# Block-sparse attention and a gated layer in one plan: another load order, wider transposes and masks, and a plan with other durations

## The chip, the cores and the metric

The kernel runs on one core of one Trainium2 chip. The core has five engines that work side by side, each with its own stream of instructions in a fixed order: PE (TensorE, matrix products; its weight loads are listed apart as PEld), DVE (VectorE), ACT (ScalarE), POOL (GpSimd) and SP (SyncE, which only issues DMAs here). They wait for each other through semaphores. PE writes to PSUM, which has eight banks of 128 partitions by 512 fp32 values; the other data lies in SBUF. DMAs are issued by SP and ACT, and by POOL where a transfer also converts fp32 to fp16.

The metric is the device time of one execution in microseconds, as the median over runs. Traces show one profiled execution, in microseconds from its first instruction.

## The reference

Four sequences (batch 4) with 8 heads, 768 positions and 64 values a head go through attention with a block mask, and the result, as 3072 tokens of 512 values, through a gated layer with 2048 hidden values.

```python
scores = scale * np.matmul(q, k.transpose(0, 1, 3, 2))
blk_i, blk_j = pos[:, None] // 32, pos[None, :] // 32
mask = np.abs(blk_i - blk_j) <= 1
mask = mask | (blk_i == 0) | (blk_j == 0) | (blk_i == 23) | (blk_j == 23)
for qb in range(24):
    for kb in sampled_blocks[qb]:          # three drawn blocks
        mask[qb*32:(qb+1)*32, kb*32:(kb+1)*32] = True
scores = np.where(mask, scores, -1e9)
attn = softmax(scores)
x = (attn @ v) as [3072, 512]
h = x @ w_in                               # [3072, 2048]
g = h * (1 / (1 + exp(-beta * h)))
out = g @ w_out                            # [3072, 512]
```

## The kernel before

**Tiling.** The 24 blocks of 32 positions of a sequence fall into two kinds. Blocks 0 and 23 see all keys ("global rows"). The other 22 see eight blocks each: three drawn ones, the first, their three neighbours and the last. They are done in 11 pairs a sequence, 44 pairs in all, named by n; g is the block within the pair, u the head within one of four head pairs hp.

**A pair's way.** `kg` on POOL (line 710) copies the six drawn key blocks into KG by offsets read from the input, `kn` (lines 714 to 732, the copy itself on the helper's line 330) the neighbours. `sc` on PE first writes the mask into two PSUM banks (line 849: a product of ones with a row that holds a large negative number where a drawn block repeats another one) and adds the scores (line 862). `mx` on DVE takes row maxima (line 884), `ex` on ACT the exponentials and their sums (line 892), `nrm` on POOL or DVE divides (line 915) from the 12th pair on; the first 11 pairs, called late, divide after the product by a factor that `hl` prepares (lines 902 to 904) and PE spreads (line 953). `tp` transposes the weights on PE (line 929; from pair 31 on by a DMA, line 933), `ptv` copies them out of PSUM, `av` multiplies by the gathered V blocks (line 971, from pair 16 on line 963), `xv` stores the result into xT.

**V.** Sequence V is rearranged into Vn, written to a table VT in DRAM (line 659), and gathered from it into VG by DMAs on SP (line 810). For the first four pairs the drawn V blocks come out of a product with a selection matrix on PE instead (`pick`, line 825). The V tiles of pairs 4 to 7 lie in g1, the second of the two buffers that later hold g.

**Preparation of a sequence.** Raw K and Q are loaded with 128 partitions of six positions each, cast to fp16 (line 538, first sequence only; the others are cast by POOL's DMAs of line 588), transposed per head pair on PE, one head at a time into half of the partitions (`trK`, `trQ`, line 632), and copied into KT and QT (`evK`, `evQ`, Q times the scale).

**Dense layers.** Tokens go in eight groups G of 256 or 512. `h` (line 1155) multiplies by w_in, `tanh` on ACT (line 1161) and `stt` on DVE (line 1166) form g, `y` (line 1182) multiplies by w_out, `oe` scales into osb, and SP stores. Weights are loaded by POOL's DMAs (lines 557, 563), which wait for a tiny POOL copy (`touch`, line 543) that waits for a V gather of pair 2.

**What sets the order.** Everything is a task in a list planner (class Plan). A task names its engine or engines, a duration, what it depends on, the banks that it opens and closes, and a priority. `Plan.run` simulates the engines, the banks and two DMA rings, and starts on each free engine the ready task of least priority plus OFFSET, a table of names. The tasks are then emitted in that order; the chip keeps it on each engine. A wrong duration does not change a result, only what stands ahead of what.

## Time and profile before

| what | value |
|---|---|
| median of 3 runs | 302.34 us (300.25 to 303.63) |
| profiled execution | span 302.9 us; no other time is given for it |
| PE busy | 279.5 us, 92% |
| DVE busy | 237.5 us, 78% |
| ACT busy | 218.6 us, 72% |
| POOL busy | 170.0 us, 56% |
| mean granted clock of PE | 0.981 |
| moved by DMA | 47.55 MB |

A row of the table of stretches gives the stretch, its length, then for PE, PEld, DVE, ACT and POOL the busy time with the count of instructions in brackets, and at the end the granted clock of PE, the share of the DMA engines and GB/s. A row of the timeline gives the start, the time from the first start to the last end, engine and line, operation, what is written and read with shapes, the count, and in brackets the idle time of the engine before it and what ended it. A row of waits names who waited for whom, the sum, the times and the longest. A row of groups has busy time and the mean of one in ns behind the first bar. PE's matmuls overlap, so a busy PE is not PE at full speed.

### The profile page before, as it was taken

To read this page: it belongs to the slowest core of one execution; us is meant where nothing else is said; L and a number is where in the kernel's file an instruction comes from. 1 tells how busy PE (TensorE), PEld (TensorE's weight loads), DVE (VectorE), ACT (ScalarE), POOL (GpSimd) and SP (SyncE) were. 2 spreads that over 40 slices of the span, in tenths; PEclk is the share of its full clock that TensorE was granted. 3 is DMA by queue.
4 is the path that set the end of the run, shared out by engine and by line. 5 is a ranking of instruction groups with operands and counts; after the bars stand their busy time and mean duration, and the time that the engine had idled before them with its cause. 6 is when DMAs were issued, how large, how long until landed. Compare 5 with 4: busy or idle time off the path is not lost.

```text
span 302.9 us, 11451 instructions
## 1 busy us (share of the span) xinstructions
PE 279.5 (92%) x4109; PEld 173.8 (57%) x4109; DVE 237.5 (78%) x556; ACT 218.6 (72%) x641; POOL 170.0 (56%) x513
## 2 busy tenths in 40 slices
PE   2599879999998799999999999999999999999993
PEld 1465668758846576665556555545554544555671
DVE  5848987999899998999999739999888834762150
ACT  3357657888789598799889749896787768763360
POOL 5057995034579957899777538677976654000000
PEclk9999957999999999999999999999999999999999
DMA  7999999979978852299933643248465446541102
GB/s 248 365 294 171 205 232 231 228 142 265 213 126 167 181 192 72 84 173 162 237 99 106 202 154 106 67 110 167 120 158 119 126 106 181 137 121 53 53 36 69
DMA packets 57170, 47.55 MB, mean 157 GB/s; under 512 B 19733, under 2 KB 53142, under 8 KB 57114
## 3 DMA queue, kind: packets, MB, share of 16 engines
q1 hardware_dynamic: 44736, 35.48, 41.3%
q0 software_dynamic: 12320, 11.27, 24.7%
q8 instruction: 32, 0.52, 0.7%
q14 instruction: 24, 0.20, 0.2%
q10 hardware_dynamic: 58, 0.07, 0.1%
HBM read 45.23 MB, written 9.44 MB: 180 GB/s over the span
## 4 chain that ended last, share of the span: by engine, by line
PE 49%; DVE 23%; issue 7%; ACT 6%; POOL 6%; DMA 5%; POOLq 2%; SPq 0%; DVEq 0%; ACTq 0%
PE bank L1155 17%; PE bank L1182 14%; DVE ST L884 5%; PE bank L825 4%; DVE g L1166 4%; PE bank L929 3%; POOL KG L710 3%; DMA g<-in_k_dram 3%; DVE SG L1040 3%; POOL PP L915 2%; PE bank L963 2%; PE bank L971 2%; ACT PP L892 2%; PE bank L632 2%; ACT t L1161 2%
## 5 line engine op out<-in xcount | busy, mean ns | idle before, releaser
L1155 PE MATMUL bank<-xT,w_in_sb 128*128 128x256 f16 (+1 forms) x512 | 93.8, 330 | 1.5 <-DVE g L1166 1.5
L892 ACT ACTIVATE PP<-bank,ST 128x256 f16<-128x256 f32 x176 | 81.9, 482 | 15.1 <-DVE ST L884 10.1
L1182 PE MATMUL bank<-w_out_sb,g 128*128 128x512 f16 x384 | 92.0, 379 | 0.0
L1161 ACT ACTIVATE t<-bank,beta_sb 128x512 f16<-128x512 f32 (+1 forms) x128 | 71.0, 595 | 15.7 <-PE bank L1155 10.4
L915 POOL TENSOR_SCALAR PP<-PP,ST 128x256 f16<-128x256 f16 x132 | 63.4, 499 | 30.8 <-DVE ST L909 29.2
L1166 DVE SCALAR_TENSOR_TENSOR g<-t,bank 128x512 f16<-128x512 f16 (+1 forms) x128 | 67.0, 547 | 16.3 <-ACT t L1161 15.8
L1155 PEld LDWEIGHTS <-w_in_sb 128*128 128x128 f16 x512 | 54.4, 115 | 28.1 <-issue 4.1
L710 POOL COPY KG<-KT 128x64 f32 x264 | 52.4, 249 | 25.6 <-PE bank L862 10.5
L884 DVE TENSOR_REDUCE ST<-bank 128x2 f32<-128x512 f32 x88 | 57.6, 680 | 4.2 <-PE bank L862 3.8
L1182 PEld LDWEIGHTS <-g 128*128 128x128 f16 x384 | 35.0, 98 | 37.4 <-issue 3.5
L892 ACT ACTIVATION_READ_ACCUMULATOR PP<-bank,ST 128x1 f32 x176 | 37.4, 212 | 0.0
L1061 POOL TENSOR_SCALAR PG<-PG,SG 128x768 f16<-128x768 f16 x13 | 13.1, 1010 | 24.4 <-ACT PG L1049 15.2
L334 ACT ACTIVATE osb<-bank 128x512 f32<-128x512 f32 (+1 forms) x24 | 14.2, 590 | 16.1 <-PE bank L1182 16.0
L330 DVE COPY PT<-bank 128x1024 f16<-128x1024 f16 x30 | 20.4, 683 | 3.8 <-PE bank L929 3.6
L330 DVE CAST xT<-bank 64x256 f16<-64x256 f32 (+1 forms) x35 | 14.6, 418 | 9.9 <-PE bank L963 6.8
L929 PE MATMUL bank<-identity,PP 128*128 128x128 f16 x248 | 20.4, 225 | 1.2 <-ACT KT L328 0.6
L963 PEld LDWEIGHTS <-VG 128*128 128x128 f16 x448 | 16.1, 98 | 9.2 <-issue 4.3
L1049 ACT ACTIVATE PG<-bank,SG 128x384 f16<-128x384 f32 x32 | 18.3, 589 | 4.2 <-DVE SG L1042 3.6
L929 PEld LDWEIGHTS <-PP 128*128 128x128 f16 x248 | 16.2, 101 | 6.0 <-issue 1.1
L963 PE MATMUL bank<-PT,VG 128*128 128x64 f16 x448 | 17.5, 193 | 2.2 <-DMA PT<-PP 1.5
L330 POOL COPY KG<-KT 128x384 f32<-128x384 f32 (+3 forms) x43 | 16.6, 411 | 1.3 <-PE bank L862 1.3
L328 ACT CAST xT<-bank 64x256 f16<-64x256 f32 (+1 forms) x30 | 11.3, 375 | 8.2 <-PE bank L1089 3.9
(119 smaller groups left out, 317.9 us busy)
## 6 DMA issues: line engine op xcount, KB each, us to landing
VG<-VT SPq DMA_DIRECT2D x220, 32.0 KB, 2.6
VG<-VT SPq DMA_DIRECT2D x32, 192.0 KB, 2.7
out_dram<-osb SPq DMA_DIRECT2D x20, 256.0 KB, 2.1
RV<-in_v_dram POOLq DMA_DIRECT2D x6, 384.0 KB, 6.6
RK<-in_k_dram POOLq DMA_DIRECT2D x6, 384.0 KB, 6.2
VT<-Vn SPq DMA_DIRECT2D x3, 768.0 KB, 3.4
RQ<-in_q_dram POOLq DMA_DIRECT2D x6, 384.0 KB, 6.3
w_in_sb<-in_moe_w_in_dram POOLq DMA_DIRECT2D x8, 256.0 KB, 8.8
```

Of the source, the lines that this page charges most:

```text
L330: (nc.vector if eng == "DVE" else nc.gpsimd).tensor_copy(out=out, in_=in_)
L710: nc.gpsimd.tensor_copy(out=kg32[:, g, :, (SR + r) * W:(SR + r + 1) * W], in_=kt32[:, :, bass.ds(vals[3 * g + r], W)])
L884: mx[n, u] = add(f"mx{n}.{u}", "DVE", 0.6, lambda n=n, u=u, sb_=sb_: nc.vector.tensor_reduce(out=sb_[:, 0, 2 * u:2 * u + 2], in_=bank(("S" ...
L892: nc.scalar.activation(out=pb[:, u, g, :], in_=bank(("S", n, u))[:, g * 256:(g + 1) * 256], func=AF.Exp, bias=sb_[:, 0, 2 * u + g:2 * u + ...
L915: (nc.vector if eng == "DVE" else nc.gpsimd).tensor_scalar(out=pb[:, u, g, :], in0=pb[:, u, g, :], scalar1=sb_[:, 2, 2 * u + g:2 * u + g + ...
L929: nc.tensor.transpose(out=o[:, s * P:(s + 1) * P], in_=pb[:, u, g, c * P:(c + 1) * P], identity=identity)
L963: nc.tensor.matmul(o[:, (g * NHP + hp) * 2 * BLK:(g * NHP + hp + 1) * 2 * BLK], lhsT=vgb[:, g, c, hp * P:(hp + 1) * P], rhs=pt[:, g, c, :, ...
L1049: nc.scalar.activation(out=pg[:, :].rearrange("x (j p) -> x j p", j=J)[:, :, hf * hw_:(hf + 1) * hw_], in_=bank(("GS", m, hf))[:, 0:S // 2 ...
L1155: nc.tensor.matmul(o[:, 0:TW], lhsT=w_in_v[:, c, f // 4, f % 4, :], rhs=xT[:, c, c0:c0 + TW], start=(c == 0), stop=(c == NHP - 1))
L1161: lambda G=G, f=f, TW=TW, tt=tt: nc.scalar.activation(out=tt[:, 0:TW], in_=bank(("H", G, f))[:, 0:TW], func=AF.Tanh, bias=0.0, scale=beta_ ...
L1166: lambda G=G, f=f, TW=TW, tt=tt, gg=gg: nc.vector.scalar_tensor_tensor(out=gg[:, f, 0:TW], in0=tt[:, 0:TW], scalar=1.0, in1=bank(("H", G, ...
L1182: nc.tensor.matmul(o[:, :], lhsT=gg[:, f, s * P:(s + 1) * P], rhs=w_out_sb[:, f, :], start=(f == 0), stop=(f == N_FFC - 1))
```

## The change

- First sequence: order of loads K, first half of Q, V, second half of Q (which waits until V's table is written); before it was V, K, Q. Q is split by partitions, K and V by heads. The casts of K and Q put the two heads of a pair beside each other and may run on DVE or ACT; Q's are eight casts of 64 partitions.
- K's transposes of that sequence take two heads at once on the full array (6 for 12 a head pair); Q's take two heads and 64 partitions at a time. Scores of the first five pairs depend on the first half of Q alone.
- Masks: two matmuls on the full array a pair for eight on 64x32 tiles.
- w_in is loaded in other pieces (one of four row groups, half of the columns), and its first half waits for V's load and not for a gather of pair 2.
- The second token group uses the second half of g0 and not g1.
- The last output is scaled by one ACT instruction and not by halves on ACT and DVE.
- The planner gets other durations, a model of PE's instruction transfers (blocks of 256), forced engines for 59 tasks (FORCE) and a new, longer table OFFSET.
- After planning, spare fp32 matmuls into a free bank are put ahead of PE tasks that the plan starts after a gap, until 50 us of the plan.

```diff
-    HOP = 0.18
+    HOP = 0.14
+    NI = {"selb": 4, "rows": 8, "maskb": 2, "betaT": 8, "pick": 12, "trK": 24, "trQ": 24, "trQa": 24, "trQb": 24,
+          "sc": 36, "tp": 16, "gs": 32, "gt": 12, "gav": 96, "h": 8, "y": 8}
+    BLOCK, FRONT, FIRST, SLOW, FAST, EASY = 256, 300, 448, 6.9, 2.6, 60.0
...
+                if e == "PE":
+                    wait = self.SLOW if now < self.EASY else self.FAST
+                    if coming is not None and coming <= now:
+                        got, coming = got + self.BLOCK, None
+                    had += t.ni
+                    while had > got:
+                        coming = now + wait if coming is None else coming
+                        t.dur = max(t.dur, coming - now)
+                        got, coming = got + self.BLOCK, None
+                    if coming is None and had > got - self.FRONT:
+                        coming = now + t.dur + wait
...
-                        end = lanes[issued % 8] = hw_at + 0.9 + (self.LATER if ring_at > hw_at else 0.0)
+                        end = lanes[issued % 8] = hw_at + 1.4 + (self.LATER if ring_at > hw_at else 0.0)
...
-    GATES = (2, 2, 2)
-    QV = (0, 2)
+    GATES = (-1, 2, 2)
...
+    COLD, UNTIL, FILL = 9.0, 50.0, 0.7
...
-                        scalar1=NEG / D, scalar2=None, op0=ALU.mult)
+                        scalar1=NEG / P, scalar2=None, op0=ALU.mult)
...
-    for z, (i, nm, t, dst) in enumerate(((2, "V", v, None), (0, "K", k, RK), (1, "Q", q, RQ))):
...
+    mixed = lambda t: t[:, :, :].rearrange("p h x -> p (h x)").rearrange("p (j m) -> p j m", j=J)
+    def cast0(eng, i, dst, hp, ps):
+        copy_on(eng, mixed(dst)[ps, :, hp * P:(hp + 1) * P].rearrange("p j (u d) -> p u j d", u=2),
+                stage_all(i)[ps, 2 * hp:2 * hp + 2, :].rearrange("p u (j d) -> p u j d", j=J))
...
+        ld0["K", f] = first("K", f, stage_half(0, f), src6(k, 0, f * HH, HH), -80 + f, 2.0 if f else 3.4)
...
+        ld0["Q", f] = first("Q", f, stage_all(1)[HALF[f]], src6(q, 0, 0, H)[HALF[f]], -78 + 4 * f)
...
+        v0ld.append(first("V", f, v_stage[:, f * HH:(f + 1) * HH, :], src6(v, 0, f * HH, HH), -77 + f))
...
+            t_win.append(add(f"win{f}.{c}", "POOL", 0.6, lambda c=c, fs=fs: nc.gpsimd.dma_start(
+                out=w_in_sb[:, c, fs], in_=w_in_r[:, c, fs]),
+                deps=[touch[f]], prio=-50 + 0.4 * f + 0.05 * c, dma=1.45, bulk=THR))
...
+                                    nc.tensor.transpose(
+                                        out=o[:, (h2 * J + j) * 64:(h2 * J + j + 1) * 64],
+                                        in_=mixed(RQ)[HALF[f], j, m:m + P],
+                                        identity=identity[HALF[f], HALF[f]], tile_position=(64 * f, 0))
...
+                    if b == 0:
+                        for j in range(J):
+                            nc.tensor.transpose(out=o[:, j * P:(j + 1) * P],
+                                                in_=mixed(s16)[:, j, hp * P:(hp + 1) * P], identity=identity)
+                        return
...
+            ld0["Q", 1].deps.append(vtab[0][1])
...
-            for hp in range(NHP):
-                for u in range(2):
-                    nc.tensor.matmul(
-                        bk[u][hp * BLK:(hp + 1) * BLK, :].rearrange(
-                            "x (g c) -> x g c", g=2)[:, :, 0:ns * BLK],
-                        lhsT=ones[u * D:(u + 1) * D, 0:BLK],
-                        rhs=maskr[u * D:(u + 1) * D, 2 * p:2 * p + 2, 0:ns].to_broadcast([D, 2, ns, BLK]),
-                        start=True, stop=False, skip_group_check=True,
-                        tile_position=(u * D, hp * BLK))
+            for u in range(2):
+                nc.tensor.matmul(
+                    bk[u][:, :].rearrange("x (g c) -> x g c", g=2)[:, :, 0:ns * BLK],
+                    lhsT=ones, rhs=maskr[:, 2 * p:2 * p + 2, 0:ns].to_broadcast([P, 2, ns, BLK]),
+                    start=True, stop=False, skip_group_check=True)
...
-        sdeps = [kg[n], kn[n], t_mask] + [evQ[b, hp] for hp in range(NHP)]
+        sdeps = [kg[n], kn[n], t_mask] + [(evQa[hp] if n < 5 else evQ[b, hp]) for hp in range(NHP)]
...
-            sc[n] = add(f"sc{n}", "PE", 0.62 if two else 0.31, lambda h=halves[n]: [f() for f in h[0::2] + h[1::2]],
+            sc[n] = add(f"sc{n}", "PE", 0.66 if two else 0.33, lambda h=halves[n]: [f() for f in h[0::2] + h[1::2]],
...
-        gi = (G + (sizes[0] < 8)) % NG if G or sizes[0] >= 8 else 0
-        gc = TW if G == 1 and sizes[0] < 8 else 0
+        gi, gc = ((0, 0), (0, 256), (1, 0), (0, 0), (1, 0), (0, 0), (1, 0), (0, 0))[G]
...
+    for t in order:
+        if t.eng != "PE":
+            continue
+        gap = t.start - at_
+        each = 0.86 if t.start < COLD else 0.43
+        k = int(FILL * gap / each)
+        if k and t.start < UNTIL:
+            calm = [(max([z for a, z in h if a < t.start - 1e-9] + [0.0]), i) for i, h in enumerate(held_at)]
+            z, i = min(calm)
+            if z < at_ + 0.1:
+                spare[t] = (i, k)
+        at_ = t.start + t.dur
+    def emit_spare(i, k):
+        for _ in range(k):
+            nc.tensor.matmul(banks[i][0:D, 0:256], lhsT=tiny, rhs=tiny.rearrange(
+                "x (a m) -> x a m", a=1).to_broadcast([P, 4, D]), start=True, stop=True, skip_group_check=True)
```

More of the change, by code (lines that the diff above doesn't have):

```diff
@@ L542 @@
[L542 to L545 removed]
+    stage_all = lambda i: g_sb[i][:, :, :].rearrange("p a b -> p (a b)").bitcast(FP32)[
+        :, 0:H * J * D].rearrange("p (h x) -> p h x", h=H)
@@ new lines @@
+    for f in range(2):
+        v0ld.append(first("V", f, v_stage[:, f * HH:(f + 1) * HH, :], src6(v, 0, f * HH, HH), -77 + f))
+    vgate = lambda n: (VGs if n < NVG else VG1)[0:1, n % NVG, 1, 1 if n < NSEL else 0, 0:1] if n >= 0 else v_stage[0:1, H - 1, 0:1]
+    touch = [add(f"touch{i}", "POOL", 0.12, lambda n=n, i=i: nc.gpsimd.tensor_copy(
+        out=(w_in_sb[0:1, 0, 0:1], w_in_sb[0:1, 0, D_FF // 2:D_FF // 2 + 1], w_out_sb[0:1, 0, 0:1])[i],
+        in_=vgate(n)), prio=-57.5 + i, deps=[v0ld[1]] if n < 0 else [])
```

183 lines of the change are left out of this document (109 added, 74 removed).

## The prediction

> **What bounds the kernel now.** I read the page first, then busy time by stretches, the waits of the matrix engine, and the timeline of the first 50 us.
>
> ```profile
> span 302.9 us, 11451 instructions
> PE 279.5 (92%) x4109; PEld 173.8 (57%) x4109; DVE 237.5 (78%) x556; ACT 218.6 (72%) x641; POOL 170.0 (56%) x513
> ...
> 0.00:10.00 10.00, 1.94 (x9) 1.06 (x9) 5.43 (x22) 2.44 (x4) 3.85 (x24) 1.00 0.80 279
> 10.00:20.00 10.00, 8.92 (x89) 6.12 (x90) 7.82 (x25) 5.09 (x7) 4.37 (x18) 1.00 1.08 344
> 30.00:40.00 10.00, 7.04 (x261) 5.18 (x259) 9.39 (x22) 7.27 (x29) 9.87 (x36) 0.93 1.18 211
> 40.00:50.00 10.00, 10.00 (x177) 8.23 (x163) 7.46 (x22) 6.01 (x24) 8.76 (x25) 0.55 1.11 233
> sum 50.00, PE 37.90 PEld 26.51 DVE 36.80 ACT 28.15 POOL 32.29; mean PE 7.58 PEld 5.30 DVE 7.36 ACT 5.63 POOL 6.46
> ...
> 50.00:62.00 12.00, 12.00 (x200) 9.17 (x198) 11.53 (x34) 9.95 (x32) 0.00 (x0) 1.00 1.17 224
> 90.00:110.00 20.00, 16.37 (x342) 11.93 (x340) 19.54 (x42) 15.93 (x51) 17.00 (x44) 1.00 0.83 189
> 110.00:140.00 30.00, 29.90 (x595) 19.70 (x590) 28.72 (x67) 26.66 (x89) 25.31 (x76) 1.00 0.50 110
> 170.00:210.00 40.00, 39.33 (x507) 21.25 (x505) 33.26 (x72) 30.27 (x94) 27.53 (x85) 1.00 0.44 122
> 210.00:252.00 42.00, 39.80 (x566) 21.46 (x565) 32.30 (x69) 31.46 (x99) 27.17 (x83) 1.00 0.56 131
> 252.00:299.00 47.00, 46.24 (x301) 26.55 (x299) 20.41 (x41) 26.32 (x56) 3.68 (x8) 1.00 0.32 91
> ```
>
> The last 47 us are the dense layers alone and PE is full there (46.24 of 47). So whatever array time PE loses earlier is paid at the end: PE's total work is the bound, and I look for what it loses. Visible idle time is 50 - 37.90 = 12.1 us before 50 us, and 3.63 + 0.10 + 0.67 + 2.20 = 6.6 us in the four later rows below 100%. VectorE (DVE) is the second bound in the middle: 19.54 of 20 and 28.72 of 30 us.
>
> Two losses hide in a busy PE. In 40 to 50 us the granted clock is 0.55, in 30 to 40 it is 0.93: a stretch of about 0.14 x 10 + 0.9 x 10 = 10.4 us at half clock, 5.2 us of array time. And the first six pick matmuls ran at half the speed of the next eighteen, though the record grants 1.00 there:
>
> ```profile
> 13.99:18.20 4.21, 2.80 (x6) 1.05 (x6) 1.00 1.10 366
> 18.20:23.40 5.20, 4.19 (x18) 2.05 (x18) 1.00 1.07 236
> ```
>
> That is 2.80 against 4.19/3 = 1.40 us, 1.4 us more. The front so loses 12.1 + 5.2 + 1.4 = 18.7 us.
>
> **Load order and first transposes.** These rows give the arrival of each half tensor, the first being whatever stands first in SP's queue.
>
> ```profile
> 5.49 0.96 DVE L330 CAST Vn<-xT 128x1536 f16<-128x1536 f32 x1 [0.94 <-DMA xT<-in_v_dram]
> 7.61 0.96 DVE L330 CAST Vn<-xT 128x1536 f16<-128x1536 f32 x1 [0.17 <-DMA xT<-in_v_dram]
> 9.70 1.03 DVE L538 CAST RK<-g 128x768 f16<-128x768 f32 x2 [0.80 <-DMA g<-in_k_dram]
> 10.32 1.49 PE L632 MATMUL bank<-identity,RK 128*64 128x128 f16 x24 [2.58 <-DVE RK L538]
> 13.88 1.03 DVE L538 CAST RQ<-g 128x768 f16<-128x768 f32 x2 [0.30 <-DMA g<-in_q_dram]
> ...
> 20.01 26.17 SPq L810 DMA_DIRECT2D g<-VT  x30
> 23.43 0.33 PE L849 MATMUL bank<-maskr,ones 64*32 64x320 f16 x8
> 44.01 1.03 PE L971 MATMUL bank<-PT,g 128*64 128x32 f16 x32
> 44.98 1.90 PE L1155 MATMUL bank<-xT,w_in_sb 128*128 128x256 f16 x8
> ```
>
> Halves arrive about 2.1 us apart (5.49, 7.61, 9.70). Put K first and its halves are there at 5.5 and 7.6, the first Q half at 9.7, V at 11.8 and 13.9 instead of 5.5 and 7.6. Casts of 0.5 us, transposes and evictions take K to about 10.4 us and Q's blocks to 12.3; six gather copies (line 710) by about 12. The first score comes at 13 us where it was 23.43. The second Q half waits behind V's two table writes, and only pairs from the sixth on need it.
>
> Earlier scores are not gained time by themselves. PE still cannot start its transposes before about 6.1 us, and it has little to do until V's picks (48 matmuls) can start near 14.9 us. Of 15 us it would fill: four K transposes of six at half clock 2.6, Q 1.2, the three first score groups 0.9, the constants' matmuls 1.9; idle 8.4, and I leave 1.5 us more until 50 us. Idle falls from 12.1 to 9.9: **-2.2 us** (0 to -2.2). The halved transposes of K and the split ones of Q are in that figure. Q's casts become eight of 64 partitions instead of four of 128: four more at 0.5 us on DVE or ScalarE, hidden in DVE's 2.2 us of idle between 10 and 20 us; uncovered, they would push the first score by 1 us with two engines sharing them.
>
> The first half of the input weights now waits for V (13.9 us) and not for a gather: its four issues stand on POOL's queue near the first gather copies, about 3 us at the 0.74 us of such an issue below. POOL is idle 5.63 us of 10 to 20 us, which covers it; uncovered, the second pair's gather is 3 us late. DMA time is full either way (share 1.08 to 1.18), so bytes change places and are not fewer.
>
> ```profile
> L557 POOL DMA_DIRECT2D w_in_sb<-in_moe_w_in_dram x8 | 5.9, 743 | 0.6 <-POOL w_out_sb L543 0.5
> ```
>
> **Filler matmuls for the clock.** They are to stand in PE's planned gaps until 50 us. If they work, 5.2 + 1.4 = 6.6 us return; if not, 0. No row shows a 256-column fp32 matmul: from below it costs 0.11 us (the forty 256-column matmuls at 286.85 below), from above the 0.43 us that the change itself plans with; a filler in a gap costs nothing while the plan's gap is real, and at most its own time where real work stands behind it. I take **-4.5 us**, two thirds, since in 10 of the 50 us DVE (9.39 of 10) set the pace too. The half clock followed a gap:
>
> ```profile
> 37.11 0.25 PE L849 MATMUL bank<-maskr,ones 64*32 64x192 f16 x1
> 39.54 0.36 PE L849 MATMUL bank<-maskr,ones 64*32 64x192 f16 x7 [2.17 <-DVE ST L884]
> ...
> q8 instruction: 1, 0.02, 1.7%
> ...
> q8 instruction: 32, 0.52, 0.7%
> ```
>
> The Trainium skill, TensorE: Matmul & The Clock Gate, Part 1, lets the clock fall to half after an idle window of about 3.4 us; here 2.4 us of silence were near the fall, so by the page this gap alone would not do it. Its Part 4 says that transposes do not count as busy in the same way; by that rule ordinary matmuls in the gaps are the right means, and the sum would be -6.6 instead.
>
> **Instruction transfers.** The gap above splits a group of eight mask matmuls after the first: not an operand's wait, whatever name the row gives, but the next block of instructions; the queue of instruction transfers moved one block in exactly that stretch (its row for 36 to 39.6 us stands first, the whole run's 32 below). It is 2.4 us, and already in the front's idle time. A plan that knows of the transfers can only reorder around them.
>
> **Masks over the whole array.** Eight mask matmuls on 64x32 tiles become two on the full array.
>
> ```profile
> 33.40 0.27 PE L849 MATMUL bank<-maskr,ones 64*32 64x192 f16 x8
> 33.48 0.40 PE L862 MATMUL bank<-KG,QT 64*32 64x256 f16 x16
> 33.70 0.27 PE L849 MATMUL bank<-maskr,ones 64*32 64x192 f16 x8
> ...
> 286.85 4.53 PE L1155 MATMUL bank<-xT,w_in_sb 128*128 128x256 f16 x40
> PEld L849 <- issue: 8.0, 20, 0.9
> ```
>
> Eight tiles take 33.48 - 33.40 = 0.08 us together, since they run side by side. A full-array matmul of 256 columns takes 4.53/40 = 0.113 us, so 192 columns some 0.085 and two of them 0.17: 0.09 us more in 36 pairs and (320 columns) about 0.14 more in eight: 3.2 + 1.1, **+4 us**. Lower end +0.9 (the change plans 0.02 us more a group, x44). Upper end: a change of tile shape cost 8.0/20 = 0.4 us before a group, and only 20 of 44 groups show it, the others following groups of the same shape; if the step from full mask to tiled score costs it in the other 24, 9.6 us more, +13.9. What is saved is 12 instructions a pair, 528 in all, two transfers.
>
> **The new plan.** Its durations, placement of copies, forced engines and priorities change nothing in the amount of work, only which instruction stands ahead of which. What can be won is waiting in order:
>
> ```profile
> POOL PG L1061 <- ACT PG L1049: 15.2, 2, 13.0
> POOL PP L915 <- DVE ST L909: 29.2, 16, 5.8
> ```
>
> POOL did nothing from 50 to 62 us because its queue's head waited 13.0 us for one exponential; the gathers behind it were late, and the chain runs over POOL from 76 to 97 us, just ahead of PE's idle 3.63 us. The new plan also puts the second token group into the first g buffer, so it need not wait for the V tiles kept in the other. Visible idle 6.6 us is what the nearest rows give; better cover of POOL's 12 us could reach 12. I take **-7 us** (0 to -12). If DVE stays 96% full in 110 to 140 us, it is what is late next. Forced engines move work between the two:
>
> ```profile
> L330 DVE COPY KG<-KT 128x768 f16<-128x768 f16 x17 | 7.4, 434 | 0.0
> ```
>
> Twelve neighbour copies are forced onto POOL, up to 12 x 0.43 = 5.2 us off DVE; nine normalisations are forced onto DVE, which the plan prices at 0.6 to 0.8 us, 5.4 to 7 us on. I cost the exchange at nothing; with DVE full, it is worth 5 us either way and stays inside the term's ends and the first two rivals.
>
> **The tail.** One ScalarE copy replaces two halves that ran one after the other.
>
> ```profile
> 294.87 0.60 ACT L334 ACTIVATE osb<-bank 128x512 f32<-128x512 f32 x1 [2.98 <-PE bank L1182]
> 298.33 0.38 ACT L334 ACTIVATE osb<-bank 128x256 f32<-128x256 f32 x1 [2.86 <-PE bank L1182]
> 298.74 0.42 DVE L336 TENSOR_SCALAR osb<-bank 128x256 f32<-128x256 f32 x1 [6.39 <-ACT osb L334]
> ```
>
> 298.74 + 0.42 - 298.33 = 0.83 against 0.60: **-0.2 us**.
>
> **Sum.** -2.2 - 4.5 + 4 - 7 - 0.2 = -9.9 us on the profiled span of 302.9, so 293.0. No other time is given for that execution; it lies 0.6 above the median 302.34, which becomes 292.4, rounded 292.5.
>
> **The rivals.** *More is won* (0.2): the clock stays up (-6.6), POOL's 12 us are used (-12), masks cost 0.9: 302.3 - 2.2 - 6.6 - 12 - 0.2 + 0.9 = 282. For it speaks that the chain crosses POOL where POOL had idled before; against it DVE at 96%. *The masks drain the array* (0.1): 9.6 us more than my sum, 302. For it the 20 waits of 0.4 us; against it that the wait is at a group's first load now, so that part of it moves and is not added. The Trainium skill, TensorEngine Tiling (Array Packing), Key Properties, says that a change of tiling mode drains the engine; the 0.4 us agree. *V comes too late* (0.15), the slower side: V lands 6.3 us later, and behind it stand the table write and SP's queue of 30 gathers, which takes 26.17 us. If those end last for pair 4, its output product moves from 44.01 to 50.3, and with it the first dense matmul. Price: 6.3 us, no gain from the plan in the front, masks +4, clock -4.5, tail -0.2: 302.3 + 6.3 + 4 - 4.5 - 0.2 = 308. It decides once V's gathers land after pair 4's transposed weights. Against it: no row of PE's waits before 50 us names a gather today. For it: the queue is still issuing at 46 us, so slack is small.
>
> **How the numbers follow.** My forecast has 0.55, with its own range 287 to 298 (masks to clock at their ends). A measurement of this kernel tells about 1% from nothing: below 299.3 is faster, above 305.4 slower. Faster is 0.52 of the forecast plus 0.2; within 1% the rest 0.03 and the drain's 0.1, less some of it that goes above; slower V's 0.15 and that part. The range 281 to 306 takes in the larger gain and the drain and leaves out most of the V case.
>
> **What would show it.** First mask or score near 13 us; a granted clock of 1.00 in every stretch to 50 us; the first dense matmul well before 44.98 us; two mask matmuls near 0.17 us a pair and no new wait named "issue" ahead of line 862's successor; POOL busy in 50 to 62 us; the stretch of dense layers alone at the end as full as now. Wrong it is if the half clock stays, if PE's idle after 50 us exceeds 6.6 us, or if PE's waits name V's gathers.

## The result and the profile after

| | before | after |
|---|---|---|
| median | 301.29 us (299.89 to 303.63) | 323.35 us (320.00 to 323.73) |
| profiled execution: time, span | -, 302.9 us | 323.6, 321.8 us |
| PE busy | 279.5 us (92%) | 292.1 us (91%) |
| first mask on PE | 23.43 us | 19.57 us |
| first gather from V's table, into VG | 16.05 us | 21.26 us |
| first gather into g | 20.01 us | 33.88 us |
| SP's last gather issued by | 269.69 us | 286.18 us |
| from there to the end of the span | 33.2 us | 35.6 us |

The changed kernel is slower: ratio 1.0696, 95% interval 1.0619 to 1.0773, about 21 us, where I had forecast 10 us less. Of 18.9 us more span, 16.5 stand ahead of the last gather of V and 2.4 behind it. PE is busy for 12.6 us more and idle for 6.3 us more. Executions of one kernel differ by about 1%: the trace of before is a long one (wherever both are known the time is about 1.8 us above the span, so its 302.9 stand for some 304.7 against the median of 301.29), and of three experiments the profiled execution was longer than the others and is not used below.

The head of the page of the changed kernel, and its table of stretches, with the columns as before (PE, PEld, DVE, ACT, POOL, granted clock, DMA share, GB/s):

```profile
span 321.8 us, 10811 instructions
...
PE 292.1 (91%) x3835; PEld 178.2 (55%) x3835; DVE 237.5 (74%) x565; ACT 230.5 (72%) x654; POOL 162.9 (51%) x494
```

```profile
0.00:10.00 10.00, 7.50 (x32) 4.18 (x33) 6.46 (x28) 5.41 (x8) 4.08 (x25) 1.00 0.82 280
...
20.00:30.00 10.00, 4.57 (x64) 2.20 (x64) 3.23 (x5) 1.35 (x5) 4.51 (x22) 0.82 1.08 248
30.00:40.00 10.00, 9.54 (x114) 5.95 (x107) 6.61 (x16) 8.85 (x28) 5.60 (x21) 0.50 0.65 112
...
50.00:62.00 12.00, 9.66 (x127) 8.03 (x127) 10.68 (x34) 10.00 (x35) 6.97 (x19) 0.86 0.93 196
...
252.00:299.00 47.00, 42.34 (x418) 22.26 (x417) 23.77 (x49) 26.76 (x70) 12.68 (x31) 1.00 0.53 113
```

Between 20 and 30 us every engine is idle more than half of the time while the DMA engines are full (1.08). The clock is at half for 2 x 0.18 x 10 + 10 = 13.6 us around there and for 2 x 0.14 x 12 = 3.4 us more after 50 us; before it was 10.4 us. In 252 to 299 us, which was the dense layers alone, GpSimd still works 12.68 us (3.68 before): attention is not done.

Of the longest pieces of the chain that ended last (start, length, what), the first three say where the front waits:

```profile
1.81 7.91 DMA xT<-in_v_dram
10.73 10.52 DMA VT<-Vn
21.26 7.31 DMA VG<-VT
```

And the timeline of 0 to 35 us, cut to the steps of V and Q:

```profile
0.75 0.47 SPq L559 DMA_DIRECT2D g<-in_k_dram  x1
...
1.27 1.04 SPq L559 DMA_DIRECT2D xT<-in_v_dram  x2
...
2.36 0.86 SPq L559 DMA_DIRECT2D g<-in_k_dram  x1
...
3.26 0.73 SPq L559 DMA_DIRECT2D g<-in_q_dram  x1
...
8.62 2.65 SPq L732 DMA_DIRECT2D VT<-Vn  x2
...
10.69 2.61 POOL L593 DMA_DIRECT2D w_in_sb<-in_moe_w_in_dram  x4
...
11.32 0.83 SPq L559 DMA_DIRECT2D g<-in_q_dram  x1
...
21.26 4.00 SPq L882 DMA_DIRECT2D VG<-VT  x6
...
23.67 0.25 PE L920 MATMUL bank<-maskr,ones 128*128 128x192 f16 x1
...
28.65 0.58 ACT L351 CAST VG<-bank 96x512 f16<-96x512 f32 x1 [9.30 <-DMA VG<-VT]
...
29.29 0.32 PE L920 MATMUL bank<-maskr,ones 128*128 128x192 f16 x1 [5.37 <-ACT VG L351]
...
31.57 2.29 ACT L351 CAST RQ<-g 64x768 f16<-64x768 f32 x3
...
33.88 0.79 SPq L882 DMA_DIRECT2D g<-VT  x2
```

Read downwards. Only one half of K goes ahead of V; the other half and Q stand behind it, so the loads do not run in the order that "The change" gives. V's halves are cast from 7.63 and 9.74 us, about 2.1 us later than before:

```profile
7.63 0.96 DVE L353 CAST Vn<-xT 128x1536 f16<-128x1536 f32 x1 [0.30 <-DMA xT<-in_v_dram]
...
9.74 0.96 DVE L353 CAST Vn<-xT 128x1536 f16<-128x1536 f32 x1 [0.56 <-DMA xT<-in_v_dram]
```

V's table write and the four loads of w_in (10.69 us) share the DMA engines, and the second half of Q joins them; the write takes 10.52 us. The gathers out of the table start at 21.26 us. ScalarE has taken a copy into VG whose tile those gathers also write, so it waits 9.30 us, and the bank that it should empty is the one the next mask needs: PE is silent for 5.4 us. Behind that copy stand the exponentials, and behind them the casts of the late half of Q (31.57 us). Those casts read the staging buffer g1, and the V blocks of pairs 4 to 7 go into that same buffer. So the first gather into g waits until 33.88 us, 13.9 us later than before.

SP's last gathers are late as well. The last group of gathers, before and after (timeline rows of the two kernels):

```profile
265.23 4.46 SPq L810 DMA_DIRECT2D VG<-VT  x9
```

```profile
281.58 4.60 SPq L882 DMA_DIRECT2D VG<-VT  x9
```

### The profile page after: what moved, and what is told of

Its sections match the earlier page's. It is cut to its first block, busy times and chain, and to the rows that moved or that the text cites. A ratio compares the mean times of both kernels' runs of the same rounds, so it can differ in the third digit from the quotient of the medians.

```text
span 321.8 us, 10811 instructions
## 1 busy us (share of the span) xinstructions
PE 292.1 (91%) x3835; PEld 178.2 (55%) x3835; DVE 237.5 (74%) x565; ACT 230.5 (72%) x654; POOL 162.9 (51%) x494
## 3 DMA queue, kind: packets, MB, share of 16 engines
q0 software_dynamic: 11296, 11.27, 23.7%
## 4 chain that ended last, share of the span: by engine, by line
PE 59%; DMA 15%; DVE 7%; SPq 7%; POOL 4%; ACT 3%; issue 3%; POOLq 1%; ACTq 0%; DVEq 0%
PE bank L1251 19%; PE bank L1224 18%; DMA VG<-VT 6%; SPq L882 4%; DMA VT<-Vn 3%; PE bank L930 3%; PE bank L998 3%; PE bank L1032 3%; DVE ST L953 3%; POOL PP L984 3%; PE bank L703 3%; DMA xT<-in_v_dram 2%; PE bank L920 2%; DMA PT<-PP 2%; PE bank L1040 2%
## 5 line engine op out<-in xcount | busy, mean ns | idle before, releaser
L1224 PE MATMUL bank<-xT,w_in_sb 128*128 128x256 f16 (+1 forms) x512 | 95.3, 332 | 2.3 <-DVE xT L1056 0.9
L1251 PE MATMUL bank<-w_out_sb,g 128*128 128x512 f16 x384 | 90.9, 380 | 0.0
L1235 DVE SCALAR_TENSOR_TENSOR g<-t,bank 128x512 f16<-128x512 f16 (+1 forms) x128 | 67.5, 549 | 26.7 <-ACT t L1230 26.1
L782 POOL COPY KG<-KT 128x64 f32 x264 | 51.1, 243 | 50.8 <-PE bank L930 33.7
L984 POOL TENSOR_SCALAR PP<-PP,ST 128x256 f16<-128x256 f16 x112 | 54.1, 500 | 28.1 <-DVE ST L978 26.0
L961 ACT ACTIVATION_READ_ACCUMULATOR PP<-bank,ST 128x1 f32 x176 | 36.7, 209 | 0.0
L357 ACT ACTIVATE osb<-bank 128x512 f32<-128x512 f32 x24 | 14.3, 602 | 20.8 <-PE bank L1251 20.7
L920 PE MATMUL bank<-maskr,ones 128*128 128x192 f16 (+1 forms) x88 | 15.2, 261 | 5.5 <-ACT VG L351 5.4
L998 PEld LDWEIGHTS <-PP 128*128 128x128 f16 x248 | 16.1, 100 | 6.8 <-issue 1.5
L930 PE MATMUL bank<-KG,QT 64*32 64x256 f16 x704 | 17.9, 280 | 1.2 <-issue 1.2
L1131 POOL TENSOR_SCALAR PG<-PG,SG 128x768 f16<-128x768 f16 x11 | 9.9, 902 | 16.7 <-DVE SG L1128 16.0
```

The source lines that it names most:

```text
L782: nc.gpsimd.tensor_copy(out=kg32[:, g, :, (SR + r) * W:(SR + r + 1) * W], in_=kt32[:, :, bass.ds(vals[3 * g + r], W)])
L930: nc.tensor.matmul(bk[u][hp * BLK:(hp + 1) * BLK, g * 256:(g + 1) * 256], lhsT=QT[b % 2][u * D:(u + 1) * D, hp, (i0 + g) * BLK:(i0 + g + 1 ...
L961: nc.scalar.activation(out=pb[:, u, g, :], in_=bank(("S", n, u))[:, g * 256:(g + 1) * 256], func=AF.Exp, bias=sb_[:, 0, 2 * u + g:2 * u + ...
L984: (nc.vector if eng == "DVE" else nc.gpsimd).tensor_scalar(out=pb[:, u, g, :], in0=pb[:, u, g, :], scalar1=sb_[:, 2, 2 * u + g:2 * u + g + ...
L998: nc.tensor.transpose(out=o[:, s * P:(s + 1) * P], in_=pb[:, u, g, c * P:(c + 1) * P], identity=identity)
L1224: nc.tensor.matmul(o[:, 0:TW], lhsT=w_in_v[:, c, f // 4, f % 4, :], rhs=xT[:, c, c0:c0 + TW], start=(c == 0), stop=(c == NHP - 1))
```

## The experiments

Each version is compared with the kernel before on the same chip. In the diffs `move` puts named tasks at another place of the planned list and `put_on` gives them another engine; everything else of the order stays. Two theories ran through them. **G, the carried lag**: the front makes V's gathers late, SP issues them in order and has too little slack to catch up, and the end follows the last gather. **L, the later order**: the new plan's order after the front costs time by itself.

The last three columns are read from each run's timeline, as in the rows above. Where they are empty, no trace is compared. In the three versions with gathers on GpSimd (a_pool, b_pool, a_windvepool) they tell of SP's gathers alone.

| run | median us | ratio [95%] | first gather VG, g | last gather by | rest of span |
|---|---|---|---|---|---|
| a_pick | 318.70 | 1.0527 [1.0434, 1.0620] | - | - | - |
| a_qb | 323.21 | 1.0691 [1.0605, 1.0778] | 26.8, 35.8 | 286.3 | 35.1 |
| a_win | 315.25 | 1.0442 [1.0340, 1.0543] | 17.8, 28.4 | 277.0 | 35.4 |
| b_hold | 314.99 | 1.0435 [1.0343, 1.0526] | 16.0, 34.0 | 279.8 | 32.9 |
| a_mask8 | 317.19 | 1.0480 [1.0416, 1.0543] | 21.9, 34.5 | 278.9 | 35.4 |
| a_nospare | 321.59 | 1.0624 [1.0561, 1.0687] | 22.1, 34.5 | 283.9 | 35.3 |
| b_full | 303.29 | 1.0032 [0.9991, 1.0072] | 16.2, 20.1 | 268.6 | 33.3 |
| a_pickwin | 317.15 | 1.0446 [1.0366, 1.0526] | 22.8, 26.7 | 281.3 | 35.6 |
| a_windve | 313.07 | 1.0420 [1.0345, 1.0496] | 17.6, 25.6 | 275.7 | 35.0 |
| a_front | 313.88 | 1.0417 [1.0344, 1.0491] | 17.9, 30.1 | 277.6 | 35.0 |
| a_frontmask | 311.88 | 1.0370 [1.0311, 1.0429] | 17.9, 27.3 | 274.9 | 35.1 |
| a_winmask | 313.58 | 1.0401 [1.0303, 1.0498] | - | - | - |
| a_qfirst | 315.90 | 1.0423 [1.0328, 1.0518] | - | - | - |
| a_qfirst2 | 313.99 | 1.0395 [1.0309, 1.0480] | 21.4, 25.5 | 277.5 | 34.9 |
| a_pool | 315.91 | 1.0447 [1.0377, 1.0518] | 22.9, 34.5 | 279.6 | 34.9 |
| b_pool | 306.45 | 1.0099 [1.0041, 1.0157] | 16.1, 20.1 | 267.7 | 36.9 |
| a_sorted | 316.65 | 1.0484 [1.0393, 1.0575] | 17.7, 25.6 | 276.5 | 35.4 |
| a_windvepool | 308.15 | 1.0203 [1.0091, 1.0314] | 17.9, 25.7 | 270.9 | 35.9 |

**The delay alone, in the old kernel.** SP is held ahead of the gathers into g (`late_sp`, all of SP's tasks between them and pair 0's result) until pair 0's result is stored; nothing else changes.

```diff
+    hold = Task("hold", "SP", 0.4, lambda: nc.sync.dma_start(out=scratch, in_=xT[0:1, 0, 0:64]))
+    at = order.index(by_name["xv0.0"]) + 1
+    order[at:at] = [hold] + late_sp
```

> The kernel before, its plan unchanged, with one tiny store on SP that reads pair 0's result, put ahead of the gathers for pair 4 and all that follows them on SP: gathers into g start at about 34 us and not at 20. Loads, masks, transposes, clock and PE's order are those of before. Theory G: all the lag of the changed kernel comes by this way, so 301.3 + 13 to 19 = 314 to 320. Rival P (PE's own losses): the queue has slack, 301 to 305.

```profile
33.95 2.06 SPq L811 DMA_DIRECT2D g<-VT  x3
...
275.36 4.48 SPq L811 DMA_DIRECT2D VG<-VT  x9
```

The gathers into g begin at 33.95 us, as in the changed kernel. Of that 13.9 us delay, 10.1 are left at the last gather (275.36 + 4.48 against 269.69), and the kernel takes 12 to 13 us more (medians 314.99 against 303.20; 0.0435 x 303.2 = 13.2). Late gathers alone, with no new plan, so cost more than half of the loss.

How the delay reaches the end is another question, and here G is not shown. In this version PE runs the same 4109 matmuls in the same order as before, so its rows can be compared one by one. PE's waits for gathers into g up to 62 us, then one row of PE before and two in b_hold:

```profile
PE bank L972 <- DMA g<-VT: 8.3, 4, 4.9
```

```profile
62.53 0.40 PE L862 MATMUL bank<-KG,QT 64*32 64x256 f16 x16
```

```profile
74.70 0.40 PE L863 MATMUL bank<-KG,QT 64*32 64x256 f16 x16
...
296.71 4.53 PE L1156 MATMUL bank<-xT,w_in_sb 128*128 128x256 f16 x40
```

At 62 us PE is already 12.2 us behind, and near the end still 9.9 (296.71 against the 286.85 of the prediction's row). After 62 us its matmuls wait only 1.7 us for any gather of V. So PE loses the time in the front, by waiting and by a lower clock (0.50 granted in 40 to 50 us and 0.78 in 50 to 62 us, against 0.55 and 1.00 before), and being idle for only 4.5 of the 190 us to 252 us it does not make it up. The late last gather can be a result of that as well as a cause.

**What makes the front late.** Three moves in the changed kernel: the table's gathers behind ScalarE's copies; the second half of Q right behind the first with its casts on VectorE; the loads of w_in's first half moved to the place of those of its second half in GpSimd's list, so that they start at 28.05 us and not at 10.69.

```diff
+    # a_pick
+    move(["vg0.0", "vg0.1", "vg0.2", "vg2.0", "vg2.1", "vg2.2"], after="pickv1.1")
+    # a_qb
+    move(["ldQ0.1"], after="ldQ0.0")
+    put_on(["castQb0.0", "castQb0.1", "castQb0.2"], "DVE")
+    # a_win
+    move(["touch0", "win0.2", "win0.0", "win0.1", "win0.3"], before="touch1")
```

> The kernel after, its plan unchanged, but the six table gathers into VG (pairs 0 to 3) are emitted behind the two ScalarE copies of picked V blocks, so that the copies no longer wait for a gather. Theory G (the end follows the start of the gathers into g, line 882, which stood at 33.88 us): the casts of Q's second half on ScalarE are then held by their data alone (27.2 us), the gathers start at about 29.5, 4.4 us earlier, and the end moves by about the same: 323.4 - 4.4 = 319. Rival P (the end follows PE's silence of 5.6 us at 23.7 and the half clock behind it): first exponential at about 21 us, no silence, no half clock of 13.7 us: -5.4 - 6 = 312. Rival N (both are covered later): 323.

> The kernel after, its plan unchanged, but the second half of Q is loaded right behind the first, ahead of the writes of V's table, and its first three casts run on VectorE and not on ScalarE. The copies of picked blocks on ScalarE still wait for the gather (28.6 us). Theory G: the gathers into g start right behind the six table gathers, at about 26.5 us and not 33.88, so the end moves by about 7: 316. Rival P (silence and half clock): those stay, so 322 to 323.

> The kernel after, its plan unchanged, but the four loads of the first half of w_in stand on POOL's queue where the second half's stand, as before the change, and not right behind V's load. If these 2 MB are what makes the table's write take 10.5 us to land and the gather 7.3: writes land near 18 us, the first gather near 24, ScalarE is free 4 to 5 us earlier, the gathers into g start at about 29: 323.4 - 5 = 318. If the loads of K and Q are what they share the DMA engines with, nothing of this moves and the first dense matmul may come later: 323 or 325.

a_win alone gives back 8 us. Its chain from 0 to 30 us and its gathers:

```profile
10.77 7.00 DMA VT<-Vn
...
17.79 5.29 DMA VG<-VT
```

```profile
28.39 7.92 SPq L882 DMA_DIRECT2D g<-VT  x11
...
272.39 4.60 SPq L882 DMA_DIRECT2D VG<-VT  x9
```

The table write takes 7.00 us instead of 10.52, the gathers land in 5.29 instead of 7.31. a_pick, in which that copy no longer waits for a gather, is worth 4 to 5 us. a_qb misses its aim:

```profile
26.81 2.81 SPq L882 DMA_DIRECT2D VG<-VT  x6
...
33.94 0.56 DVE L353 CAST RQ<-g 64x768 f16<-64x768 f32 x1
...
35.22 0.57 DVE L353 CAST RQ<-g 64x768 f16<-64x768 f32 x1
```

With the second half of Q ahead of it the table write ends 5.5 us later still, and the last two casts run at 33.94 and 35.22 us, now behind other work in VectorE's queue. The gathers start later and the time is unchanged.

**Masks and fillers.** Masks back on eight tiles; no fillers; and the two full-array masks alone in the old kernel.

```diff
+    # a_mask8: the eight 64x32 mask matmuls of the kernel before, NEG / D
+    # a_nospare
-    COLD, UNTIL, FILL = 9.0, 50.0, 0.7
+    COLD, UNTIL, FILL = 9.0, 0.0, 0.7
+    # b_full: the kernel before with the two full-array mask matmuls, NEG / P
```

> The kernel after, its plan unchanged, with the masks as before: eight matmuls on 64x32 tiles for two on the full array, and 528 instructions more on PE. If the full-array masks cost what two streams of 192 columns cost over eight side by side (0.09 us a pair, 4 us), and PE is the bound: 323.4 - 4 = 319. If each score group now pays a change of tile shape that it did not pay before (0.4 us in about 24 groups): 323.4 - 13 = 310. Theory G (the gathers set the end, PE has room until the dense layers stand alone): within 1 us of 323.

> The kernel after, its plan unchanged, without the filler matmuls. Theory G: 323, within 1. If the fillers keep the clock up at all, the first picks run at half speed again and the end is 1 to 3 us later. If they stand in the way of real matmuls, it is 1 to 2 us earlier.

> The kernel before, its plan unchanged, with the full-array masks alone (two matmuls for eight, 528 instructions fewer). By the sum of the prediction: 302 + 4 = 306; with a change of tile shape in each group 315; if PE waits for gathers at that place anyway, 302.

In the old kernel the wide masks cost 1.0 us, from -0.3 to +2.2. In the changed one, tiled masks give 6 us back, where theory G had them within 1 us of nothing. The groups of mask matmuls, after and in a_mask8 (busy time, mean ns), explain 2.9 of them:

```profile
L920 PE MATMUL bank<-maskr,ones 128*128 128x192 f16 (+1 forms) x88 | 15.2, 261 | 5.5 <-ACT VG L351 5.4
```

```profile
L921 PE MATMUL bank<-maskr,ones 64*32 64x192 f16 (+1 forms) x352 | 12.3, 266 | 4.4 <-ACT VG L351 4.4
```

The other 3 us aren't explained. In the mended versions the same step was worth 2 us or less (a_front to a_frontmask, a_win to a_winmask, fillers taken out as well, intervals overlapping), so I don't read 6 us as the price of a mask. Taking the fillers out gave 1.8 us, inside the intervals. All fourteen stand ahead of 11 us:

```profile
1.51 1.11 PE L1318 MATMUL bank<-ones 128*64 128x256 f32 x2 [1.51 <-POOL ones L368]
5.24 1.11 PE L1318 MATMUL bank<-ones 128*64 128x256 f32 x2
7.88 3.06 PE L1318 MATMUL bank<-ones 128*64 128x256 f32 x10
```

They fill gaps that the plan foresaw. It did not foresee the silence at 23.7 us, none stands there, and there the clock fell.

**How much of the front comes back together.** The moves combined: a_pick with a_win; a_win with all late Q casts on VectorE (a_windve); that with V ahead of all of K (a_front); with tiled masks and no fillers (a_frontmask; a_winmask is a_win with these two).

```diff
+    # a_windve: a_win and
+    put_on(["castQb0.0", "castQb0.1", "castQb0.2"], "DVE")
+    move(["castQb0.0", "castQb0.1", "castQb0.2"], after="castQb0.3")
+    # a_front: a_windve and
+    move(["ldK0.0"], after="ldV0.1")
+    move(["vperm0.0"], before="sel16.0")
```

> The kernel after, its plan unchanged, with both: the six table gathers behind ScalarE's two copies of picked blocks, and the first half of w_in loaded where the second half is. Theory G: the gathers into g start when Q's second half is there (23.5 us with w_in late) and cast on ScalarE, at about 26.5 instead of 28.4 with w_in late alone, so the end is 2 us earlier than that run: 313. If the two gains were independent (4.7 and 8.1 us): 310.6. What is left over 302 is then not in the front alone.

> The kernel after, its plan unchanged, with the first half of w_in loaded where the second half is, and the four casts of Q's second half all on VectorE, one behind the other. Theory G (the lag of SP's gathers at the 20th is the lag of the end, within 3 us): with w_in late alone the gathers into g started at 28.4 because ScalarE cast from 26.1; on VectorE they start at about 25.7, so 315.3 - 2.7 = 312.5. Rival L (with w_in late the front no longer sets the end, later places of the plan do): 315.

> As the run before, and V's two halves are loaded ahead of all of K, as in the kernel before. V's table is written 2 us earlier, and the gathers into g start at 21 to 23 us, 1 to 3 behind the kernel before. Theory G: the end comes 2 to 5 us behind that of before: 305 to 308. Rival L: what is lost after 60 us stays, 313 to 315.

> As the run before, and masks on eight tiles again and no fillers, so that of the change only the split of Q, the plan and the second group's buffer are left. Masks and fillers alone were worth 6.2 and 1.8 us in the plan after: if these add up with the front, 298 to 300, and if they are only chance of order, the same as the run before.

> The kernel after, its plan unchanged, w_in's first half late, masks on eight tiles, no fillers. If the three are independent: 323.4 - 8.1 - 6.2 - 1.8 = 307. If they all lead through SP's gathers (start at about 28 us): 312 to 315.

The gains don't add. a_front missed its aim: its gathers into g came at 30.1 us and not at 21 to 23. a_pickwin has earlier gathers into g than a_win (26.7 against 28.4 us) and later ones into VG, and is no faster. All the others end between 312 and 314 us. In a_windve the clock stayed up in the front, and still 12 us remain:

```profile
30.00:40.00 10.00, 9.07 (x233) 6.20 (x233) 9.30 (x25) 9.55 (x36) 9.68 (x34) 1.00 1.06 194
40.00:50.00 10.00, 7.26 (x110) 5.83 (x111) 9.56 (x33) 9.85 (x36) 7.00 (x26) 1.00 1.09 228
```

So the half clock isn't what remains here; whether it cost part of the 10 us that came back isn't shown. In the three of these with full columns the last gather comes by 274.9 to 277.6 us, and the end 35.0 or 35.1 us later.

**The front in the old order.** Both halves of Q ahead of the table write, casts ahead of the first maxima, with V first (a_qfirst) or behind half of K (a_qfirst2).

```diff
+    # both: a_win and
+    move(["ldQ0.1"], after="ldQ0.0")
+    put_on(["castQb0.0", "castQb0.1", "castQb0.2"], "DVE")
+    move(["castQb0.0", "castQb0.1", "castQb0.2", "castQb0.3"], before="mx0.0")
+    # a_qfirst also
+    move(["ldK0.0"], after="ldV0.1")
+    move(["vperm0.0"], before="sel16.0")
```

> The changed kernel with the front brought back near the old order: V ahead of all of K, the second half of Q right behind the first on SP, its casts on VectorE ahead of the first row maxima, the input weights' first half issued behind V's gathers' gate. Carried-lag theory (the delay of V's gathers at the front is handed through SP's queue to the end, and the end follows the last gather by about 35 us): first gather into g at 20 to 22 us, last gather 2 to 5 us later than in the kernel before, 303 to 307 us. Rival (the new plan's later order costs about 10 us of its own): the first gather is just as early, the lag grows again after 60 us, 311 us or more.

> The same, but V stays behind the first half of K, as in the changed kernel. Carried-lag theory: first gather into g 0 to 2 us later than in the run with V first, and 304 to 309 us. Rival: 311 us or more, as in the run with V first.

Neither theory's condition was met: in a_qfirst2 the early Q pushed the table write, the gathers into VG began at 21.4 us, those into g stood behind them at 25.5, and the last came by 277.5 us. The end again came 35 us behind the last gather, but that doesn't tell whether a fully restored front would be enough. No version got both kinds of gathers back to 16 and 20 us. V ahead of K brought nothing either: a_qfirst is no faster than a_qfirst2.

**Issues taken off SP.** From pair 12 on the neighbour gathers, 38 of them, are issued by GpSimd at the same places of the list.

```diff
-                (nc.sync if eng == "SP" else nc.gpsimd).dma_start(out=o, in_=i)
+                (nc.gpsimd if where == 1 and n >= 12 else nc.sync).dma_start(out=o, in_=i)
```

> The changed kernel with the neighbour gathers of V from pair 12 on (about 38 gathers) issued by GpSimd at the same places of the plan, so SP issues some 17 us less at 0.45 us each. If SP's rate of issue keeps the lag alive: the last gather on SP comes 5 to 12 us earlier and the time is 311 to 318 us. If the gathers are paced by buffers that come free and SP only passes them on: 321 to 325 us. If GpSimd's own queue (0.74 us an issue) delays the key gathers: over 326 us.

> The kernel before with the same gathers on GpSimd. If SP's rate of issue bounds the end there too: 296 to 300 us. If it does not: 301 to 304 us. If GpSimd's queue suffers: over 305 us.

> The same starting run with the neighbour gathers of V from pair 12 on issued by GpSimd. In the changed kernel itself this took 8 us off. If SP's rate of issue still holds the end here: 305 to 309 us. If that gain was only catching up a lag that this run no longer has: 311 to 314 us.

In the changed kernel this gives 7 us with the front as late as ever (gathers into g at 34.5 us), so SP's rate of issue costs time there. It shows at the end: from 252 us on PE is idle for 9.5 us in the changed kernel and for 5.0 in a_pool (4.7 before), and PE's waits for gathers into VG go from 4.7 us in seven to 1.8 us in two. On top of a_windve it gives another 5 us (6.5 by the ratios) and ends at 308.15 us, 1.0203 of before, the best version found:

```profile
25.66 10.11 SPq L882 DMA_DIRECT2D g<-VT  x14
...
267.27 3.60 SPq L882 DMA_DIRECT2D VG<-VT  x6
```

```profile
L882 POOL DMA_DIRECT2D VG<-VT x38 | 24.4, 644 | 6.5 <-PE bank L1032 6.5
```

GpSimd pays 24.4 us for them, which it has. In the old kernel, whose gathers aren't late, the same move costs 3 us: SP ends 2 us earlier, but the work behind it takes 36.9 instead of 33.2 us. GpSimd was busier there (170 against 163 us).

**SP's own order.** On a_windve, the gathers from pair 13 on in the order of their pairs; the new plan had mixed neighbours (parts of pair 26 ahead of 25, 22 and 23 interleaved).

```diff
+    # SP tasks vgN.*, vvN with N >= 13: same slots, sorted by N, no earlier than what they wait for
```

> The run with the input weights early and the late Q casts on VectorE (313.1 us), and in addition SP's gathers of V from pair 13 on in the order of their pairs; the new plan has put gathers of later pairs ahead of those of earlier ones there. The lag of its gathers against the kernel before was about nothing at the 140th gather and 6 us at the last. If SP's own order makes that growth: last gather at 270 to 273 us instead of 275.3, and 307 to 311 us. If the order on the computing engines makes it (buffers come free late): last gather unchanged and 312 to 314 us.

Neither came earlier: the last gather by 276.49 us against 275.69, and 316.65 us. Putting SP's gathers in order does not bring the rest back.

## Why the prediction was wrong

**What bounds the kernel.** I took PE's total work as the bound, and lost array time as paid at the end. In b_hold that is what happens: what PE loses in the front stays lost. What it left out is the queue that feeds PE with V, at the front and for the last pairs. PE's idle time in us, as the stretch less PE's busy time in it:

| | 0 to 62 us | 62 to 252 us | 252 us to the end |
|---|---|---|---|
| before | 12.1 | 6.6 | 4.7 |
| b_hold | 20.8 | 4.5 | 4.8 |
| after | 13.0 | 7.2 | 9.5 |
| a_pool | 15.0 | 4.6 | 5.0 |
| a_windve | 10.0 | 5.0 | 8.4 |
| a_windvepool | 8.3 | 3.9 | 5.9 |

In the changed kernel's front, 5.3 us of fillers (1.11 + 1.11 + 3.06) stand as busy time beside the 13.0. Of the 12.6 us that PE is busy longer, these fillers, 2.9 us of masks and, as an estimate, half of 6.6 us more at half clock make 11.5. The late V thus costs in two places: in the front, where PE cannot make it up, and behind 252 us, where fewer issues on SP take most of it away.

In the changed kernel SP issues 272 gathers into VG and, from pair 31 on, one transposing DMA a pair (minimum, median and maximum in ns, first and last start in us):

```profile
L882 SPq DMA_DIRECT2D VG<-VT x272: 315/369/2083, 21.3 to 285.8; - x136
```

```profile
L1002 SPq DMA_TRANSPOSE PT<-PP x13: 1231/1259/2399, 215.9 to 279.1; - x13
```

Both kernels have this stream, and in every version with full columns above the end came 32.9 to 36.9 us behind SP's last gather. That alone proves no cause, since a gather also waits for a buffer that PE must free. The queue was in my own text ("SP's queue of 30 gathers"), as a cost at the front; I didn't ask what it does for the last pairs.

**Load order, -2.2 us: the step that failed.** It took the new order as a gain of 2.2 us in the front; what the runs show are late gathers of V that cost several times as much. Two of its premises were wrong, and both could be read from the change. The order K, Q, V was taken from the priorities in the loop, but the new OFFSET table has 'ldK0.1': 151 and 'ldQ0.0': 154, which put them behind V again; V was 2.1 us later and not 6.3, and the first mask came at 19.57 us and not near 13. And "only pairs from the sixth on need" the second half of Q is right for scores and wrong for memory: it is staged in g1, where the V blocks of pairs 4 to 7 belong. With w_in moved ahead ("bytes change places", costed at nothing while GpSimd's queue had room) the step cost about 8 us by a_win alone, and a delay of the gathers into g as long as here costs 12 to 13 us in the old kernel (b_hold). The cover that I named was GpSimd's time; what was short was the DMA engines, whose share of 1.08 to 1.18 I quoted in the next sentence.

**V comes too late, the rival with 0.15,** is nearest to what happened, though not by the path that I gave. The first gather into g came 13.9 us later than before, and pair 4's output product at 59.45 us where it was 44.01. But up to 62 us no wait of PE names a gather into g: the first dense matmul stands ahead of that product in the new order, and PE waited 5.4 us for ScalarE's copy, which waited for a gather into VG. That the product was late because of its gathers is not shown. Behind 62 us PE's waits do name V's gathers:

```profile
PE bank L1032 <- DMA VG<-VT: 4.7, 7, 1.3
```

Its size was off: I moved the first dense matmul from 44.98 to 51.3 at most (6.3 us); it came at 53.05, and 16.5 us were there at the last gather.

**Fillers, -4.5.** One part came true, the 1.4 us of the first picks. In the changed kernel the first four take 1.06 us; without the fillers (a_nospare) they take 1.87, as they did before (1.94):

```profile
10.87 1.06 PE L897 MATMUL bank<-Vn,xT 128*96 128x512 f16 x4
```

```profile
10.81 1.87 PE L897 MATMUL bank<-Vn,xT 128*96 128x512 f16 x4 [2.91 <-DVE Vn L353]
```

In the whole it gained nothing: the kernel without fillers is no slower, and PE stood still for 5.4 us soon after. The other part did not come: the clock stayed at half 6.6 us longer than before, and no filler stood where the silence was. Without fillers it was not down for longer (granted 0.91, 0.74, 0.83 and 0.86 from 20 to 62 us in a_nospare). By the Trainium skill, TensorE: Matmul & The Clock Gate, Part 1, the clock falls after an idle window of about 3.4 us. The silence of 5.4 us here is longer than that, but the clock fell some 2.5 us into it (granted 1.00 up to 26 us, 0.69 in 26 to 27 us), and in the kernel before it fell within a silence of 2.2 us (37.36 to 39.54 us; I had read 2.4). That the half clock then held for 13.6 us, with PE 9.54 of 10 us busy in most of it, is not told by that rule. The first four fillers also took more than my upper end, 1.11/2 = 0.55 us apiece for 0.43; the other ten took 0.31.

**Masks, +4.** Right in sign; the busy rows give +2.9, and the time of the old kernel moved by 1.0 us (-0.3 to +2.2), at the lower end of my range. The drain rival (9.6 us more) falls: the waits named "issue" at the step between mask and score are as long in sum in b_full as they were before (8.0 us in 20 waits):

```profile
PEld L858 <- issue: 8.4, 39, 1.2
```

Line 858 is the scores' line in b_full. These waits came twice as often and were half as long.

**The new plan, -7.** Nothing of it was seen. GpSimd does work in 50 to 62 us now (6.97 us where it was 0.00), but PE's idle time from 62 to 252 us is 7.2 us, and it was 6.6. With the front's largest faults mended (a_windve) the span is still 7.8 us over that of before, 6.0 of it ahead of the last gather and 1.8 behind. Its fillers and wide masks are not the whole of it: without both, and with V ahead of K (a_frontmask), PE is busy for 280.1 us, as before, but idle for 29.8 us and not 23.4. Taking issues off SP recovers about half. How the rest divides between the front's remaining lateness (25.6 against 20.0 us) and the order of the other engines stays open; sorting SP's gathers did not recover it.

**Tail, -0.2.** Right: from the start of the last scaling to the output's issue 317.58 - 316.96 = 0.62 us, before 299.20 - 298.33 = 0.87.

```profile
316.96 0.60 ACT L357 ACTIVATE osb<-bank 128x512 f32<-128x512 f32 x1 [2.85 <-PE bank L1251]
317.58 0.33 SPq L1270 DMA_DIRECT2D out_dram<-osb  x1
```

```profile
299.20 0.33 SPq L1206 DMA_DIRECT2D out_dram<-osb  x1
```

**Sum.** I took the span of 302.9 us for a time, 0.6 above the median. With the 1.8 us between span and time it was some 2.4 above. The forecast of 292.5 is the same, since the -9.9 come off the median either way.

## What to carry to other kernels

A queue that issues in order all through the kernel can bound it at places even if no busy row shows it: look at the first and the last of its issues. Price a late start by what the fullest engine loses until it is served, since an engine with little idle time afterwards does not make it up; and when two lags run together, follow the same instructions of both engines through the two traces before calling one the cause. When a load is moved, follow its staging buffer to the next thing that is written there, and read the planner's whole table for its name before believing the order that the loop suggests. Filling planned gaps does not help against an unplanned wait.

## What the runs showed of the hardware

- The second of the two DMAs that write V's first table landed in 7.00 us in a_win and in 10.52 us with GpSimd's four weight loads beside it; the first gathers behind it took 5.29 and 7.31 us.
- Spreading issues paid here only where the issuing queue was late: 38 gathers moved from SP to GpSimd gave 7 and 5 us in the changed versions and cost 3 us in the old kernel. The Trainium skill, DMA: Bandwidth & Descriptors, Issuing engines are not separate DMA queues, says that this saves only the sequencer's time for issuing, usually small beside the transfer; 7 us of 323 are the measurement here.
- Two full-array masks and eight tiled ones wait about equally long in sum at the change of shape (8.4 us in b_full and 8.0 before, in the waits named "issue").
